# Two token tiles of batch 0 multiplied as a pair, by seven half-size products in place of two plain tiles

## The chip, the core and the metric

The kernel runs on one core of one Trainium2 chip. The metric is the device time of one execution in microseconds; the number given for a kernel is the median of several runs. Engines are called as the profile calls them: PE (TensorE, matrix products), PEld (its weight loads, which run beside it), DVE (VectorE), ACT (ScalarE), POOL (GpSimd) and SP (SyncE). POOL and SP also issue transfers (DMA). Each engine works through a queue of its own in order; where it needs something from another, it waits at that instruction, and all that is queued behind it waits too.

## The reference

There are four batches of 768 tokens. Each goes through a sparse attention of 8 heads of width 64, whose result is a row of 512 numbers for each of the 3072 tokens; then through a feed-forward part with 2048 inner numbers:

```python
# attention, per head (S=768, D=64): near keys within 16 tokens, and one summary key per block of 32
k_sum = k.reshape(B, H, nb, 32, D).max(axis=3)
v_sum = v.reshape(B, H, nb, 32, D).mean(axis=3)
scores_all = concat([where(|i-j| < 16, q @ k.T / sqrt(D), -1e9), q @ k_sum.T / sqrt(D) + log(32)])
a = softmax(scores_all)
attn = a @ concat([v, v_sum])
# feed-forward
x = attn as (3072, 512)
h = x @ w_in                                  # (3072, 2048)
g = h * (1 / (1 + exp(-1.702 * h)))
out = g @ w_out                               # (3072, 512)
```

## The kernel before, in words

The work goes in units. Batch 0 is two units of 384 tokens each (its two halves), batches 1 to 3 are one unit each. For a unit the kernel first forms the inner numbers: 16 ff tiles of 128 inner numbers each (`ff_in` for batch 0, lines 640 to 647), four matrix products of 128x128 by 384 tokens for each tile, then the gelu on ACT, which writes a row `nt` of `gT`. A batch has 6 token tiles of 128 tokens; the left half holds three, the right half the other three. Then it forms the output: for each token tile all 16 rows of `gT` times `w_out`.

Two ways of forming the output are in the kernel. `ff_out` (lines 848 to 859) is the plain one: 16 products of 512 columns into one PSUM bank `po`, in four parts of four products; ACT copies the bank to SBUF (`osb`) and SP stores it. `product` (lines 760 to 824) is used for batches 1 to 3: a pair of token tiles (one left, one right) is taken together, in seven steps of eight products of 256 columns each instead of the eight that four quarter blocks would need (Strassen's scheme in Winograd's form). It needs sums and differences of the two tiles' inner numbers, `gs` (four of them, made by `g_sums`, lines 668 to 675), and of the blocks of `w_out`, `ws` (`w_sum`, lines 679 to 686). The seven go to three banks `poA`, `poC` and `poB`. Between them intermediate values are copied out (`s1` after product 1, `s5` after 5, `s2` after 6), and later results are a bank plus such a copy, added on DVE into `osb` (after products 2, 7 and 3); the last quarter is a copy by ACT (after product 4). Product 6 goes on adding onto the bank that `s1` was copied from, 7 onto the one that `s2` was copied from, and 4 onto the one that the sum of 7 was read from, so each has to wait for that copy or sum.

The stage of interest is batch 0's right half (its second unit), lines 1079 to 1096. While its ff tiles are formed (line 1083 on), a table `todo` puts work for batch 1's attention in between: `tk` and `tq` transpose keys and queries on PE (the key copies go to ACT, the query copies to DVE; a key's maxima `ks` are reduced on DVE and spread by POOL in `rest_k`), `w_sum` forms parts of `ws` on DVE, and `value_rows(1)` at the end sums the value blocks on PE into two banks `ps_vs`, from which DVE makes `vs`. Then come 12 slots (line 1090): each is a part of `ff_out`, and then what `plan1` lists for that slot of batch 1's attention: `s` scores of one head pair and the exponential on ACT, `m` the mask on DVE, `v` values and their norms on DVE, `x` transposes of the result, `t` the query transposes t2 and t3, `g` a switch of ACT's table. Two digits name the half and the head pair or group. In slot 2 POOL is given batch 2's loads, after slots 9 and 11 SP is given transposing loads of keys (`xk`).

All instructions are kept in the order of the program on each engine (class `_Ordered`, lines 18 to 32), so no planner moves them; what the framework still chooses is which free bank a tile gets and which waits are set. PSUM has eight banks: the pool `pmm` has four, used by ff tiles, `po`, the `poA`-like banks, query transposes, `ps_vs` and batch 1's values (two for each group); the pool `psb` has two double ones, for scores, key transposes and the result's transposes.

The lines that the change touches are 668 to 675 (a neighbour is added), 760 to 824, the table `plan1` in lines 1010 to 1012 and lines 1083 to 1096. The order of ff tiles named in it, `order2`, is the one that the later batches use: 0, 8, 1, 9, and so on (line 649).

Of the kernel before, what the change touches and what calls it, by code (L numbers as in the profile page):

```python
# [13 lines left out]
ALU = mybir.AluOpType  # L14
# [21 lines left out]
def kernel(  # L36
# [15 lines left out]
    d_model, d_ff = moe_w_in.shape  # L52
# [6 lines left out]
    NT = d_ff // 128  # L59
    HALF = S // 2  # L60
    TH = NQ // 2
    JH = NJ // 2

    pe = _Ordered(tc, nc.tensor)
    dve = _Ordered(tc, nc.vector)
# [139 lines left out]
    gTb = keep.tile([128, NT, S], F16, name="gT")  # L205
# [48 lines left out]
    def copy(eng, out, in_):  # L254
        if eng is act:
            act.activation(out=out, in_=in_, func=ACT.Copy)
        elif eng == "dve_alone":

            dve.tensor_reduce(out=out, in_=in_.unsqueeze(len(in_.shape)), axis=AX.X, op=ALU.max)
        else:  # L260
            eng.tensor_copy(out=out, in_=in_)
# [278 lines left out]
    def tk(p, s, eng):  # L540
        ps = psb.tile([128, 2048], BF16, name="ps_t", tag="big")[:, 0:S]
        turn_tiles(ps, kb2[p // 2][:, p % 2], NJ)
        copy(eng, at(flat_kx(p, s), 0, [[256, NJ], [192, 2], [1, 64]]),
             ps.rearrange("p (j e c) -> p j e c", e=2, c=64))
        rest_k(p, s, pool)
# [82 lines left out]
    def gelu(half, nt, ph):  # L628
        act.activation(out=gT[half][:, nt, :], in_=ph, func=ACT.Gelu_apprx_sigmoid)
# [3 lines left out]
    def ff_step(ph, half, nt, steps=range(KO)):  # L633
        for n in steps:
            g, i = n // 2, n % 2
            ko = g + 2 * i if halves[0] else 2 * g + i
            pe.matmul(out=ph, lhsT=w_in_sb[:, ko, nt * 128:(nt + 1) * 128],
                      rhs=xTT[half][g][:, i], start=(n == 0), stop=(n == KO - 1))

    def ff_in(half, nts):  # L640

        phs = [pmm.tile([128, HALF], F32, name="ph", tag="mm") for nt in nts]
        for part in ((0, 1), (2, 3)):
            for nt, ph in zip(nts, phs):
                ff_step(ph, half, nt, part)
        for nt, ph in zip(nts, phs):
            gelu(half, nt, ph)

    order2 = [nt for j in range(NT // 2) for nt in (j, j + NT // 2)]
# [18 lines left out]
    def g_sums(j, eng=dve, which=(0, 1, 2, 3)):  # L668
# [3 lines left out]
        for w in which:  # L672
            a, b_, op = {0: (a1[:, r], a2[:, r], ALU.add), 1: (gs[:, 0, j], a1[:, l], ALU.subtract),
                         2: (a1[:, l], a1[:, r], ALU.subtract), 3: (a2[:, l], gs[:, 1, j], ALU.subtract)}[w]
            eng.tensor_tensor(out=gs[:, w, j], in0=a, in1=b_, op=op)

    N1 = d_model // 2

    def w_sum(what, part):

        n = NT // 2
        c = slice(part * n // 2, (part + 1) * n // 2)
        w1, w2 = w_out_sb[:, 0:n], w_out_sb[:, n:]
        b11, b12, b21, b22 = w1[:, c, 0:N1], w1[:, c, N1:], w2[:, c, 0:N1], w2[:, c, N1:]
        a, b = {0: (b12, b11), 1: (b22, ws[:, 0, c]), 2: (b22, b12), 3: (b21, ws[:, 1, c])}[what]
        dve.tensor_tensor(out=ws[:, what, c], in0=a, in1=b, op=ALU.subtract)
# [31 lines left out]
    def last_bank(tag, name):  # L718
        return plast[tag in "AB"].tile([128, 512], F32, name=name, tag="last" + tag,
                                       bufs={"A": 3, "E": 2, "B": 1, "C": 2}[tag])  # L720
# [36 lines left out]
        gelu("CBAE".index(bank) % 2, j + (NT // 2 if bank in "AE" else 0), ff_now[j, bank])  # L757


    def product(b, t, what):  # L760
        n = NT // 2
        l = slice(t * 128, t * 128 + 128)
        r = slice(HALF + t * 128, HALF + t * 128 + 128)
        lo, hi = slice(0, N1), slice(N1, d_model)
        raw_l, raw_r = gTb[:, :, l], gTb[:, :, r]
        w1, w2 = w_out_sb[:, 0:n], w_out_sb[:, n:]
        lhs, rhs, bank, opens = {
            1: (raw_l[:, 0:n], w1[:, :, lo], "A", True),
            2: (raw_l[:, n:], w2[:, :, lo], "C", True),
            6: (gs[:, 1, :, l], ws[:, 1], "A", False),  # L770
            5: (gs[:, 0, :, l], ws[:, 0], "B", True),
            7: (gs[:, 2, :, l], ws[:, 2], "A", False),
            3: (gs[:, 3, :, l], w2[:, :, hi], "B", False),
            4: (raw_r[:, n:], ws[:, 3], "A", False)}[what]
        if opens:
            now[t, bank] = (last_bank("B" if bank == "A" and t == 2 else {"A": "A", "B": "E", "C": "C"}[bank],
                                      "po" + bank) if b + 1 == B
                            else pmm.tile([128, 512], F32, name="po" + bank, tag="mm"))
        po = now[t, bank][:, 0:N1]
        for i in range(n):  # L780
            pe.matmul(out=po, lhsT=lhs[:, i], rhs=rhs[:, i], start=(opens and i == 0),
                      stop=(i == n - 1), skip_group_check=True)

        def keep_it(name):
            if b + 1 == B and name == "s1":
                t_ = now[t, name] = spare[:, 2 * HALF + t * N1:2 * HALF + (t + 1) * N1]
            else:
                t_ = now[t, name] = snap.tile([128, N1], F32, name=name, tag=name)
            copy(dve if t == 0 and b + 1 < B else act, t_, po)

        def give(o, cols, name):
            if (t, o) not in now:
                now[t, o] = outp.tile([128, d_model], F32, name="osb", tag="osb")
            if name:
                dve.tensor_tensor(out=now[t, o][:, cols], in0=po, in1=now[t, name], op=ALU.add)
            else:
                act.activation(out=now[t, o][:, cols], in_=po, func=ACT.Copy)

        def store(o, tok, cols=slice(0, d_model)):
            r0 = b * S + tok  # L800
            sp.dma_start(out=out[r0:r0 + 128, cols], in_=now[t, o][:, cols])
            if cols.start == 0:
                now.pop((t, o))

        last = b == B - 1 and t == JH - 1

        if what == 1:
            keep_it("s1")
        elif what == 2:
            give("o1", lo, "s1")  # L810
        elif what == 6:
            keep_it("s2")
        elif what == 5:
            keep_it("s5")
        elif what == 7:
            give("o2", hi, "s5")
            if last:
                store("o2", HALF + t * 128, hi)
        elif what == 3:
            give("o1", hi, "s2")  # L820
            store("o1", t * 128)
        else:
            give("o2", lo, None)
            store("o2", HALF + t * 128, lo if last else slice(0, d_model))

    seq = [(0, 1)]
    for t in range(JH):
# [20 lines left out]
    def ff_out(u, ms, part):  # L848
        if part == 0:
            po_now[ms] = pmm.tile([128, d_model], F32, name="po", tag="mm")  # L850
        po = po_now[ms]
        for nt in range(4 * part, 4 * part + 4):
            pe.matmul(out=po, lhsT=gT[u % 2][:, nt, ms * 128:(ms + 1) * 128],
                      rhs=w_out_sb[:, nt, :], start=(nt == 0), stop=(nt == NT - 1))
        if part == 3:
            osb = outp.tile([128, d_model], F32, name="osb", tag="osb")
            act.activation(out=osb, in_=po, func=ACT.Copy)
            r0 = u * HALF + ms * 128
            sp.dma_start(out=out[r0:r0 + 128, :], in_=osb)
# [10 lines left out]
    def exp_soon():  # L870
        act.activation(out=gate[:, 1:2], in_=gate[:, 0:1], func=ACT.Exp)
# [120 lines left out]
    for e in range(2):  # L992
        r = slice(64 * e, 64 * e + 64)
# [5 lines left out]
    for p in range(NP):  # L999
# [9 lines left out]

    plan1 = {-1: ["s00", "s01"], 1: ["t2", "m00", "m01"], 2: ["t3", "s02"], 3: ["s03", "m02"], 4: ["m03", "s10"],  # L1010
             5: ["s11", "m10"], 6: ["v00", "m11", "s12", "s13"], 7: ["v01", "g"], 8: ["m12", "m13"],
             9: ["x00", "x01", "v10"], 10: ["v11"], 11: ["x10"]}

    plan = {-1: ["s00", "s01"], 2: ["m00", "m01"], 3: ["s02", "s03"], 5: ["m02", "m03", "s10", "s11"],
            7: ["m10", "m11", "s12", "s13"], 9: ["m12", "m13"], 10: ["v00", "v01"], 11: ["d00"],
# [52 lines left out]
    gs = snap.tile([128, 4, NT // 2, HALF], F16, name="gs")  # L1068
    ws = keep.tile([128, 4, NT // 2, N1], F16, name="ws")
    exp_soon()  # L1070
    beside0(-1)
    for i, (ms, part) in enumerate((ms, part) for part in range(4) for ms in range(JH)):
        ff_out(0, ms, part)
        beside0(i)
        if i in (10, 11):
# [3 lines left out]
    todo = {3: [lambda: tk(0, 1, act)], 4: [lambda: w_sum(2, 0)], 5: [lambda: tk(1, 1, act)],  # L1079
            6: [lambda: w_sum(2, 1)], 7: [lambda: w_sum(3, 0)], 8: [lambda: tk(2, 1, act)],   # L1080
            10: [lambda: w_sum(3, 1)], 9: [lambda: tq(0, 1, dve)], 11: [lambda: tk(3, 1, act)], 12: [lambda: tq(1, 1, dve)],
            15: [lambda: value_rows(1)]}
    ff_in(1, range(3))
    for nt in range(3, NT):
        ff_in(1, (nt,))
        for f in todo.get(nt, ()):
            f()
    exp_soon()
    beside(1, -1)
    for i, (ms, part) in enumerate((ms, part) for ms in range(JH) for part in range(4)):  # L1090
        ff_out(1, ms, part)
        beside(1, i)
        if i == 2:
            load_batch(2)
        if i in (9, 11):
            xk(i // 2 - 4, 0)


# [1 line left out]
    for b in range(1, B - 1):  # L1100
# [32 lines left out]
        i = 0  # L1133
# [16 lines left out]
    b, n = B - 1, NT // 2  # L1150
# [25 lines left out]
    for slot in range(7 * (n - PLAIN)):  # L1176
# [3 lines left out]
        for j in range(PLAIN, n):  # L1180
            for what in steps.get(slot - 7 * (j - PLAIN), ()):
                ff_do(j, what)
    ff_do(n - 2, "A")
    product(b, 0, 1)
    ff_do(n - 1, 7)
    ff_do(n - 1, "c")
# [45 lines left out]
```

## Time and profile before

| | before |
|---|---|
| time, median of 3 runs | 208.15 us (207.64 to 208.67) |
| span of the profiled execution, first to last instruction | 205.6 us |
| granted TensorE clock in it | 1.000 |
| PE busy | 198.5 us, 97% |
| DVE busy | 139.9 us, 68% |
| ACT busy | 123.7 us, 60% |
| POOL busy | 93.5 us, 45% |

The profile gives no time of its own for the profiled execution beside the span; the median of the runs is 2.55 us above that span.

How to read it: the profile is of one execution. A line of the order of time gives start, duration from the first start to the last end of a merged group, engine, operation, what is written and from what, and the count. Starts are from the first instruction on. Successive matrix products overlap, so a group's pace is read from starts and not from the durations of single products. A value in square brackets is the time for which the engine stood idle before the group, and what released it. The chain that ended last gives 90% of its time to PE.

### The profile page before, as it was taken

Reading aid. Unit: us, or ns where it says so; the run is one execution under the profiler, and the core shown is the slowest. Engines: PE = TensorE matmul, PEld = TensorE weight load, DVE = VectorE, ACT = ScalarE, POOL = GpSimd, SP = SyncE. Lnnn points to the kernel's source line nnn. Section 1 sums busy time; section 2 is a strip of 40 time slices with the busy share of each in tenths; the row PEclk is TensorE's granted clock in tenths of the full one; section 3 lists DMA queues with packets and bytes.
Section 4 is the critical chain, followed back from the end, with each engine's and each line's share of the span. In section 5 each row is a group of like instructions: output and inputs, shape, how many; then the busy total and the mean of one; then the engine's idle time right before and its main releaser. Section 6 shows DMA issues by size and latency. Waiting matters only on the chain.

```text
span 205.6 us, 5854 instructions
## 1 busy us (share of the span) xinstructions
PE 198.5 (97%) x2364; PEld 138.1 (67%) x2364; DVE 139.9 (68%) x388; ACT 123.7 (60%) x237; POOL 93.5 (45%) x145
## 2 busy tenths in 40 slices
PE   7889999999999999999999999999999999999992
PEld 7658564556754566565888875566888865668882
DVE  4767795594856793898757789896769546758221
ACT  2374975728885716677772446778670577983220
POOL 7976289645899585000977036000000019990000
PEclk9999999999999999999999999999999999999999
DMA  5999999999999999999999989999023640000223
GB/s 59 153 158 198 207 212 207 204 156 233 124 145 153 177 170 135 163 145 141 139 180 158 164 162 136 130 248 154 0 105 86 149 126 3 0 0 3 102 102 105
DMA packets 97131, 27.74 MB, mean 135 GB/s; under 512 B 86720, under 2 KB 94160, under 8 KB 97104
## 3 DMA queue, kind: packets, MB, share of 16 engines
q0 software_dynamic: 71472, 13.64, 90.7%
q1 hardware_dynamic: 25632, 13.74, 32.3%
q8 instruction: 18, 0.29, 0.7%
q14 instruction: 9, 0.07, 0.1%
HBM read 27.26 MB, written 6.29 MB: 163 GB/s over the span
## 4 chain that ended last, share of the span: by engine, by line
PE 90%; DMA 4%; POOL 3%; issue 1%; DVE 1%; ACT 0%; POOLq 0%; DVEq 0%
PE ph L28 33%; PE poA L28 16%; PE po L28 11%; PE poB L28 8%; PE ps_av L28 4%; DMA v0n<-in_v_dram 4%; PE poC L28 4%; PE phA L28 4%; PE ps_s L28 3%; PE ps_t L28 1%; POOL kb L28 1%; PE ps_x L28 1%; PE phB L28 1%; PE phC L28 1%; PE phE L28 1%; PE ps_vs L28 1%
## 5 line engine op out<-in xcount | busy, mean ns | idle before, releaser
L28 PE MATMUL ph<-xT,w_in_sb 128*128 128x384 f16 x416 | 70.2, 326 | 0.1
L28 PEld LDWEIGHTS <-w_in_sb 128*128 128x128 f16 x452 | 43.7, 98 | 27.8 <-issue 0.2
L28 ACT ACTIVATE gT<-ph 128x384 f16<-128x384 f32 x104 | 49.8, 491 | 18.5 <-PE ph L28 18.2
L28 PEld LDWEIGHTS <-gT 128*128 128x128 f16 x312 | 28.8, 98 | 11.0
L28 ACT ACTIVATE a_sb<-ps_s 128x768 bf16<-128x768 f32 (+1 forms) x32 | 25.0, 826 | 12.7 <-PE ps_s L28 12.7
L28 PEld LDWEIGHTS <-gs 128*128 128x128 f16 x288 | 27.7, 98 | 3.4
L28 POOL DMA_DIRECT2D vw<-in_v_dram x36 | 24.5, 694 | 12.0 <-DMA kb<-in_k_dram 6.3
L28 POOL TENSOR_TENSOR gs<-gT 128x384 f16<-128x384 f16 x9 | 8.2, 909 | 42.4 <-ACT gT L28 42.4
L28 PE MATMUL po<-w_out_sb,gT 128*128 128x512 f16 x96 | 23.6, 380 | 0.0
L28 DVE TENSOR_TENSOR a_sb<-a_sb,mk 128x768 bf16<-128x768 bf16 x28 | 14.9, 555 | 6.5 <-ACT a_sb L28 5.9
L28 PE MATMUL poA<-ws,gs 128*128 128x256 f16 x144 | 18.7, 273 | 0.0
L28 DVE TENSOR_TENSOR x<-ps_av,rc 128x384 f16<-128x384 f32 x32 | 17.8, 558 | 1.1
L28 DVE TENSOR_TENSOR gs<-gT 128x384 f16<-128x384 f16 (+1 forms) x34 | 13.4, 393 | 7.2 <-ACT gT L28 6.9
L28 POOL DMA_DIRECT2D qb<-in_q_dram x18 | 16.6, 936 | 1.9 <-DMA w_in_sb<-in_moe_w_in_dram 1.2
L28 POOL DMA_DIRECT2D kb<-in_k_dram x16 | 15.3, 970 | 1.2 <-POOLq L1216 0.8
L28 PEld LDWEIGHTS <-kx 64*128 64x128 bf16 (+1 forms) x372 | 9.4, 95 | 6.8 <-issue 4.4
L28 DVE TENSOR_REDUCE ks<-kx 128x24 bf16<-128x768 bf16 x12 | 11.4, 948 | 3.4 <-ACT kx L28 3.2
L28 ACT ACT_TABLE_LOAD x10 | 12.8, 1283 | 1.0 <-PEq L1216 0.8
L28 ACT ACTIVATE osb<-poA 128x256 f32<-128x256 f32 x9 | 3.5, 384 | 15.8 <-PE poA L28 15.8
L28 ACT ACTIVATE s<-poA 128x256 f32<-128x256 f32 x11 | 4.2, 385 | 11.2 <-PE poA L28 11.2
L28 PEld LDWEIGHTS <-a_sb 128*64 128x64 bf16 (+2 forms) x400 | 7.8, 108 | 2.8 <-issue 1.3
L28 PE MATMUL poA<-w_out_sb,gT 128*128 128x256 f16 x72 | 9.4, 273 | 0.0
(113 smaller groups left out, 281.4 us busy)
## 6 DMA issues: line engine op xcount, KB each, us to landing
out_dram<-osb SPq DMA_DIRECT2D x23, 256.0 KB, 3.7
kb<-in_k_dram POOLq DMA_DIRECT2D x16, 192.0 KB, 6.9
qb<-in_q_dram POOLq DMA_DIRECT2D x14, 192.0 KB, 9.2
vw<-in_v_dram POOLq DMA_DIRECT2D x36, 64.0 KB, 5.7
w_out_sb<-in_moe_w_out_dram POOLq DMA_DIRECT2D x4, 512.0 KB, 13.0
w_in_sb<-in_moe_w_in_dram POOLq DMA_DIRECT2D x3, 512.0 KB, 12.7
vw<-vs SPq DMA_DIRECT2D x6, 198.0 KB, 7.1
v0n<-in_v_dram POOLq DMA_DIRECT2D x4, 192.0 KB, 7.9
```

Of the source, the lines that this page charges most:

```text
L28: r = f(*a, **kw)
```

## The change

Batch 0's right half has three token tiles. Before, each is formed by `ff_out`. After, the last two (the fifth and sixth of the batch) are formed as a pair by `product` in seven steps, in the order 1, 2, 5, 6, 7, 3, 4, and then the first of the three by `ff_out` in four parts; that makes 11 slots for 12. `product` is given the two tiles' numbers, and reads the sums from columns 0 to 127 of `gs`. The sums come from a new function, `g_sums_tiles`, which forms all four for two rows and their partners at once; it is called on DVE behind ff tiles 5, 9 and 13 of the order and behind the first product. So that partners are there early, the ff tiles of this half are formed in the order `order2`. The slot of `x10` moves from 11 to 10, and `xk` from after slots 9 and 11 to after slots 8 and 10.

```diff
+    def g_sums_tiles(j, L, R, eng):
+        js, js2 = slice(j, j + 2), slice(j + NT // 2, j + NT // 2 + 2)
+        l, r = slice(L * 128, L * 128 + 128), slice(R * 128, R * 128 + 128)
+        o = [gs[:, w, js, 0:128] for w in range(4)]
+        for w, (a, b_, op) in enumerate(((gTb[:, js, r], gTb[:, js2, r], ALU.add), (o[0], gTb[:, js, l], ALU.subtract),
+                                         (gTb[:, js, l], gTb[:, js, r], ALU.subtract),
+                                         (gTb[:, js2, l], o[1], ALU.subtract))):
+            eng.tensor_tensor(out=o[w], in0=a, in1=b_, op=op)
...
-    def product(b, t, what):
+    def product(b, t, what, tiles=None):
         n = NT // 2
-        l = slice(t * 128, t * 128 + 128)
-        r = slice(HALF + t * 128, HALF + t * 128 + 128)
+        L, R = tiles or (t, JH + t)
+        l = slice(0, 128) if tiles else slice(t * 128, t * 128 + 128)
+        ll, r = slice(L * 128, L * 128 + 128), slice(R * 128, R * 128 + 128)
         lo, hi = slice(0, N1), slice(N1, d_model)
-        raw_l, raw_r = gTb[:, :, l], gTb[:, :, r]
+        raw_l, raw_r = gTb[:, :, ll], gTb[:, :, r]
...
-             9: ["x00", "x01", "v10"], 10: ["v11"], 11: ["x10"]}
+             9: ["x00", "x01", "v10"], 10: ["v11", "x10"]}
...
-    ff_in(1, range(3))
-    for nt in range(3, NT):
-        ff_in(1, (nt,))
-        for f in todo.get(nt, ()):
+    ff_in(1, order2[0:3])
+    for i in range(3, NT):
+        ff_in(1, (order2[i],))
+        for f in todo.get(i, ()):
             f()
+        if i in (5, 9, 13):
+            g_sums_tiles((i - 5) // 2, JH + 1, JH + 2, dve)
     exp_soon()
     beside(1, -1)
-    for i, (ms, part) in enumerate((ms, part) for ms in range(JH) for part in range(4)):
-        ff_out(1, ms, part)
+    steps1 = [("seven", what) for what in (1, 2, 5, 6, 7, 3, 4)] + [("plain", part) for part in range(4)]
+    for i, (kind, what) in enumerate(steps1):
+        if kind == "plain":
+            ff_out(1, 0, what)
+        else:
+            product(0, 1, what, (JH + 1, JH + 2))
+        if i == 0:
+            g_sums_tiles(6, JH + 1, JH + 2, dve)
         beside(1, i)
         if i == 2:
             load_batch(2)
-        if i in (9, 11):
+        if i in (8, 10):
             xk(i // 2 - 4, 0)
```

The stores inside `product` use `L * 128` and `R * 128` in place of `t * 128` and `HALF + t * 128`.

More of the change, by code (lines that the diff above doesn't have):

```diff
@@ L817, in product @@
             if last:
-                store("o2", HALF + t * 128, hi)
+                store("o2", R * 128, hi)
         elif what == 3:
             give("o1", hi, "s2")
-            store("o1", t * 128)
+            store("o1", L * 128)
         else:
             give("o2", lo, None)
-            store("o2", HALF + t * 128, lo if last else slice(0, d_model))
+            store("o2", R * 128, lo if last else slice(0, d_model))
     seq = [(0, 1)]
```

## The prediction

> **What bounds the kernel now.** I read three views: first the page's busy times, then the table of windows over the stage that the change touches, then the order of time of each engine in it. The page's first part:
>
> ```profile
> PE 198.5 (97%) x2364; PEld 138.1 (67%) x2364; DVE 139.9 (68%) x388; ACT 123.7 (60%) x237; POOL 93.5 (45%) x145
> ```
>
> TensorE (PE) is busy for 97% of the span of 205.6 us, so a microsecond taken from it or added as a wait in front of it counts nearly in full. The windows of the stage (window, its length, then busy time of PE, PEld, DVE, ACT, POOL):
>
> ```profile
> 52.30:58.30 6.00, 6.00 (x54) 3.98 (x51) 4.75 (x8) 4.68 (x10) 5.26 (x13) 1.00 1.81 117
> 67.90:72.10 4.20, 4.20 (x86) 2.45 (x86) 3.63 (x10) 3.28 (x4) 1.77 (x3) 1.00 2.14 187
> ```
>
> PE has no gap worth naming, at a granted clock of 1.00. VectorE (DVE) is the next engine: 4.75 of 6.00 us in the ff stage ahead, 3.63 of 4.20 us later. That is where added work can turn into waits. The order of time on PE (start, duration of the merged group, operation, count):
>
> ```profile
> 58.30 0.60 PE L28 MATMUL ps_vs<-vw,E 64*32 64x128 bf16 x48
> 59.30 1.90 PE L28 MATMUL po<-w_out_sb,gT 128*128 128x512 f16 x8
> 61.29 0.49 PE L28 MATMUL ps_t<-wide,qb 128*128 128x128 bf16 x6
> 62.91 0.35 PE L28 MATMUL ps_s<-qT,kx 64*128 64x64 bf16 x12
> 63.20 1.04 PE L28 MATMUL po<-w_out_sb,gT 128*128 128x512 f16 x4
> ...
> 74.81 1.04 PE L28 MATMUL po<-w_out_sb,gT 128*128 128x512 f16 x4
> 75.69 0.50 PE L28 MATMUL ps_x<-ident,x 128*128 128x128 f16 x6
> 76.02 1.46 PE L28 MATMUL ph<-xT,w_in_sb 128*128 128x384 f16 x8
> 81.65 0.60 PE L28 MATMUL ps_vs<-vw,E 64*32 64x128 bf16 x48
> ```
>
> A slot of four 512-wide products lasts 0.87 us (four starts of 0.217, worked out below; 74.81 to 75.69 is 0.88); a slot's twelve score products take 0.29 (62.91 to 63.20).
>
> **The change part by part.**
>
> *The products.* Out: two tiles of 16 products, 32 x 0.217 = 6.94 us. In: seven groups of eight 256-wide ones. Their price stands in the chain of the later batches, which do the same, and that of a 512-wide one in its row of least, median and greatest duration:
>
> ```profile
> 98.41 0.98 PE poA L28 x8
> 99.39 0.87 PE poB L28 x8
> ```
>
> ```profile
> L28 PE MATMUL po<-w_out_sb,gT x96: 379/379/390, 31.1 to 75.5; 128*128 128x512 f16 x96
> ```
>
> 0.87 us is 0.109 each, 56 x 0.109 = 6.10 us; after attention work a group takes 0.10 more (0.98), as plain slots do. So one half-size product costs as much as one slot of four plain ones; there are 11 slots for 12, and the gain is one slot: -0.88 us. The row of 59.30 gives 0.217 for 512 columns as (1.90 - 0.379)/7, that is 2.0 times the 256-wide price. The Trainium skill ("TensorE: Matmul & The Clock Gate", Back-to-back issue gap) gives sustained 131 ns at 512 columns and 81 ns at 128, by which 32 plain ones would cost 4.2 us, the 56 some 5.5 us (an estimate between its two figures), and the change would lose 1.3 us on PE alone; this trace shows 217 ns and contradicts it.
>
> *The sums on DVE ahead of the stage.* Four groups of four 256-element sums come in, three of them into the ff stage. The nearest rows are the same sums over 384 elements, and a 1024-element one for the slope:
>
> ```profile
> 80.98 0.36 DVE L28 TENSOR_TENSOR gs<-gT 128x384 f16<-128x384 f16 x1 [2.56 <-ACT gT L28]
> 81.37 0.36 DVE L28 TENSOR_TENSOR gs<-gs,gT 128x384 f16<-128x384 f16 x1
> 81.65 0.35 DVE L28 TENSOR_TENSOR gs<-gT 128x384 f16<-128x384 f16 x1
> 81.92 0.35 DVE L28 TENSOR_TENSOR gs<-gT,gs 128x384 f16<-128x384 f16 x1
> ```
>
> The ff stage of DVE now, which they join:
>
> ```profile
> 52.33 0.68 DVE L28 TENSOR_TENSOR ws<-w_out_sb 128x1024 f16<-128x1024 f16 x1
> 52.93 0.68 DVE L28 TENSOR_TENSOR ws<-w_out_sb,ws 128x1024 f16<-128x1024 f16 x1
> 53.75 0.95 DVE L28 TENSOR_REDUCE ks<-kx 128x24 bf16<-128x768 bf16 x1
> 54.62 0.55 DVE L28 COPY qT<-ps_t 128x768 bf16<-128x768 bf16 x1
> 55.08 0.68 DVE L28 TENSOR_TENSOR ws<-w_out_sb,ws 128x1024 f16<-128x1024 f16 x1
> 56.37 0.95 DVE L28 TENSOR_REDUCE ks<-kx 128x24 bf16<-128x768 bf16 x1 [0.60 <-ACT kx L28]
> 57.24 0.55 DVE L28 COPY qT<-ps_t 128x768 bf16<-128x768 bf16 x1
> 59.09 0.29 DVE L28 COPY vpart<-ps_vs 128x128 f32<-128x128 f32 x1 [1.30 <-PE ps_vs L28]
> 59.41 1.18 DVE L28 TENSOR_TENSOR vs<-ps_vs,vpart 32x128 bf16<-32x128 f32 x4
> ```
>
> From start to start a group of 384 is 0.39 + 0.28 + 0.27 + 0.27 = 1.21 us. 1024 elements start 0.60 apart and 384 start 0.27 apart, 0.52 ns an element, so 128 fewer save 0.066 each: 0.95 us a group. The first group goes in at 52.33, ahead of that row. DVE's spare time is 0.22 us before 53.75 (52.93 + 0.60) and 0.69 before 56.37 (55.08 + 0.60), so two groups leave it 1.90 - 0.91 = 0.99 us late at 57.24: the copy of the second q transposes ends at 58.78 instead of 57.79. The second ps_vs bank is that copy's bank (the program's list of waits has it so), and ps_vs is due at 58.30: it slips by about 0.5.
>
> *POOL beside them.* From 56.47 on POOL copies keys, the first and last of its rows:
>
> ```profile
> 56.47 0.74 POOL L28 COPY kx<-kx 128x80 bf16<-128x80 bf16 x3
> 60.30 0.43 POOL L28 COPY kx<-ks 128x288 bf16<-128x288 bf16 x1
> ```
>
> Near the end of the run stand two rows that show what that can do:
>
> ```profile
> 184.64 0.91 POOL L28 TENSOR_TENSOR gs<-gs,gT 128x384 f16<-128x384 f16 x1
> 185.09 0.67 DVE L28 TENSOR_TENSOR gs<-gT 128x384 f16<-128x384 f16 x1 [0.66 <-ACT gT L28]
> ```
>
> The same DVE sum, 0.36 alone, took 0.67 when it began inside a POOL operation and ended 0.21 after it. The sixteen POOL copies fill 56.47 to 60.73, 0.27 each. Six DVE operations with two inputs from SBUF now fall among them: the last of the second group, the 1024-wide one moved there from 55.08, and the third group's four. Each waits between 0 and a whole copy; I take half, 0.13, as nothing in the trace orders the two queues. That makes the copy end at 59.04 and ps_vs start at 59.07, the third group run from 58.95 to 60.43, vpart start at 60.43 (for 59.09), and vs give DVE back at 61.85 (0.32 and four of some 0.28 behind it). The fourth group, 0.95, ends at 62.80. The Trainium skill ("SBUF — State Buffer", Who interferes with whom) says that a DVE instruction with two SBUF inputs and a GpSimd instruction that reads SBUF exclude each other for the whole instruction; by that, the two alternate and every wait is nearer a whole copy, which is the second rival. The 0.67 row agrees.
>
> *The first result add stands ahead of the q copy.* On DVE the sum osb<-poC is queued before the copy of t2, which scores s02 need. Its other input, s1, comes from ScalarE (ACT) behind the two exponentials:
>
> ```profile
> 60.32 1.49 ACT L28 ACTIVATE a_sb<-ps_s 128x768 bf16<-128x768 f32 x2
> ```
>
> One copy and one add take (least, median and greatest duration in ns):
>
> ```profile
> L28 ACT ACTIVATE s<-poA x11: 383/384/392, 106.0 to 198.5; 128x256 f32<-128x256 f32 x11
> L28 DVE TENSOR_TENSOR osb<-poC,s x6: 418/424/426, 102.5 to 162.0; 128x256 f32<-128x256 f32 x6
> ```
>
> s1 is ready at 61.81 + 0.38 = 62.19, so the add can go at 62.23 at the earliest; with DVE's lateness it goes at 62.80, the copy runs from 63.14 to 63.70, s02 starts at 63.73. Before it was 62.91: **+0.82 us**. PE's own work would have reached s02 at about 63.6, so the waits at ps_vs (0.77) and here are one delay and not two, and the 0.25 for which PE stood before 61.29 is used up by it.
>
> *s03 and the chain over one bank.* Two masks and the copy of t3 follow on DVE (starts 0.46, 0.47, 0.47 apart, as above between 54.62 and 55.08), which ends at 65.09; s03 starts at 65.12 instead of 64.99. Product 7 adds onto the bank that s2 is copied from, and only s03 lies between 6 and 7: product 6 ends at 64.89, the copy runs from 65.10 to 65.48, product 7 starts at 65.51 instead of 65.28. **+0.23 us** for both. The later batches have product 2 in that place. Products 3 and 4 wait for nothing: their copies and adds (0.38 and 0.42) lie 1.2 us ahead.
>
> *One slot fewer at the end.* **-0.88 us**. But x10 now follows v11 at once. It needs the norms of v10:
>
> ```profile
> 74.47 0.56 DVE L28 TENSOR_TENSOR x<-ps_av,rc 128x384 f16<-128x384 f32 x1
> 75.85 0.56 DVE L28 TENSOR_TENSOR x<-ps_av,rc 128x384 f16<-128x384 f32 x1
> ```
>
> They end 75.03; x10 began at 75.69, and without the slot would at 74.81: **+0.25 us** of wait. The fourth ff bank of the next batch is then wanted at 76.37 and free with the last norm at 76.41: **+0.05**.
>
> *At nothing.* The order of ff tiles: same products, same widths. ACT's three copies and one eviction of 0.38 for two evictions of 0.60: it is idle for more than a fifth of the windows above (4.68 of 6.00, 3.28 of 4.20 us busy). POOL's queue keeps its order, SP's its count of stores (three); the key transposes move one slot earlier behind them. If loads and stores collide otherwise than now, it shows at 81.65, where the last value loads land:
>
> ```profile
> L28 POOL DMA_DIRECT2D vw<-in_v_dram x2: 684/690/697, 74.5 to 75.2; - x2
> DMA to landing us min/median/max: 6.7/6.9/7.1
> ```
>
> 75.2 + 6.7 = 81.9, and ps_vs, begun at 81.65, uses that row in its last sixth, at 82.0. With PE half a microsecond later, and POOL's copies, hence these loads, late by as much, I take 0, with up to 0.5 either way.
>
> **The sum**: 0.82 + 0.23 - 0.88 + 0.25 + 0.05 = +0.47 us. The span becomes 206.1; the page gives no time of its own for that execution beyond the span, and the median of the runs, 208.15, lies 2.55 above it, so 208.15 + 0.47 = 208.6.
>
> **The rivals.**
>
> *The waits are covered* (208.1). No contention with POOL: ps_vs at 58.81, vpart 59.64, the add at 62.23 as ACT allows, s02 at 63.15, +0.24 in place of +0.82, a sum of -0.11. For it: the POOL copies are short. Against: the 0.67 row.
>
> *DVE and POOL alternate* (209.5; slower). Each of the six operations waits a whole copy, 0.27: vpart 61.23, the add 63.6, s02 64.52, +1.61, a sum of about +1.3. It decides, that is passes half a per cent, from a mean wait of 0.22. A group price of 1.21, as at 384 elements, does it too with half the waits. For it: the 0.67 row; against: POOL's operation there was 0.91 long.
>
> *The whole slot is gained* (207.3). It needs every wait gone, and besides the loads: a PE earlier by 0.88 stands before the row that lands at 81.9 and keeps about 0.1 only, so that even a perfect stage would end near 208.0. That is the change not doing what it says, by a transfer, and I count it with the covered case.
>
> **How the numbers follow.** The forecast (208.3 to 209.1) has 0.45; covered, or given back at the loads, 0.28; alternation 0.22; the whole slot 0.05. The prediction is the likeliest, 208.6. Range 207.8 to 209.7: from the covered case less 0.3 of the runs' own spread up to the alternation. Half a per cent is 1.04 us, about what a measurement can tell: above 209.19 lies most of alternation and the top of the forecast, 0.22; below 207.11 hardly anything, 0.03; 0.75 between.
>
> **What would show it.** Right: seven half-size products at 0.87, the first ps_vs start near 59.1, DVE's osb<-poC near 62.8 followed by the q copy, PE idle before s02, before product 7 and before x10, and the next batch's first ph near 76.5 (76.02 + 0.47). The sums among POOL's copies should show durations over 0.30. Wrong: no idle at s02 (then DVE was not late, and 208.1 is nearer), ps_vs past 59.3 or a first ph past 77 (alternation), or a gap at the next ps_vs that outweighs the stage.

## The result and the profile after

The changed kernel is slower: the ratio to the kernel before is 1.0085 (95% interval 1.0065 to 1.0106), which on 208.15 us is 209.9. Over twenty runs of each on the same chips the medians are 210.08 us (207.96 to 214.12) and 207.84 us (206.78 to 209.87); the ratio leaves out a few executions that ran at a disturbed pace and are in these medians. On 207.84 us the ratio gives 209.6. The profiled execution took 209.56 us with a span of 207.9 us (205.6 before). The forecast was 208.6, in a range of 207.8 to 209.7, with 0.75 on "within half a per cent" and 0.22 on "slower"; 0.85% is outside that half per cent.

The page's first part and its shares of the chain that ended last, for the changed kernel:

```profile
PE 198.6 (96%) x2388; PEld 140.9 (68%) x2388; DVE 144.6 (70%) x407; ACT 124.2 (60%) x239; POOL 93.8 (45%) x145
PE 57%; DMA 20%; POOL 17%; issue 4%; DVE 0%; ACT 0%; POOLq 0%; DVEq 0%
```

PE is busy for 198.6 us, as before (198.5), in a span that is 2.3 longer: the loss is not more work for PE but waiting. The chain is no longer PE's alone; 20% of it is now transfers and 17% POOL. The chain in order of time says which (start, length, what):

```profile
56.15 2.95 POOL kx L28 x9
...
73.11 2.68 POOL vw L28 x4
75.79 8.40 DMA vw<-in_v_dram
...
84.23 0.25 PE ps_vs L28 x7
```

It goes from POOL's key copies through its loads to the last value load of batch 2, which takes 8.40 us to land, and only then to PE. Now the order of time on PE; the stage begins 0.27 us earlier in this execution (58.03 for 58.30), so 0.27 has to be added to compare with before:

```profile
58.03 0.23 PE L28 MATMUL ps_vs<-vw,E 64*32 64x128 bf16 x1
58.62 0.59 PE L28 MATMUL ps_vs<-vw,E 64*32 64x128 bf16 x47 [0.36 <-DVE qT L28]
...
62.92 0.49 PE L28 MATMUL ps_t<-wide,qb 128*128 128x128 bf16 x6 [0.19 <-DVE osb L28]
63.48 0.35 PE L28 MATMUL ps_s<-qT,kx 64*128 64x64 bf16 x12
...
64.79 0.35 PE L28 MATMUL ps_s<-qT,kx 64*128 64x64 bf16 x12
65.28 1.03 PE L28 MATMUL poA<-ws,gs 128*128 128x256 f16 x8
...
75.94 0.51 PE L28 MATMUL ps_x<-ident,x 128*128 128x128 f16 x6 [0.20 <-DVE x L28]
76.28 1.54 PE L28 MATMUL ph<-xT,w_in_sb 128*128 128x384 f16 x8
...
81.99 0.85 PE L28 MATMUL ps_vs<-vw,E 64*32 64x128 bf16 x41
84.23 0.25 PE L28 MATMUL ps_vs<-vw,E 64*32 64x128 bf16 x7 [1.39 <-DMA vw<-in_v_dram]
84.41 1.80 PE L28 MATMUL ph<-xT,w_in_sb 128*128 128x384 f16 x10
```

In the kernel before, ph goes on behind the second ps_vs (which begins at 81.65) at once:

```profile
82.18 0.66 PE L28 MATMUL ph<-xT,w_in_sb 128*128 128x384 f16 x3
```

From the first ps_vs to the next batch's first ph it is 76.28 - 58.03 = 18.25 us, for 17.72 before (76.02 - 58.30): the stage lost 0.53. The second ps_vs is reached 23.96 after the first (23.35 before), 0.61 late. Then its last seven products wait 1.39 us for value loads, and ph goes on 2.42 after ps_vs began, for 0.53 before (82.18 - 81.65): 1.89 more in one place. Together that is 2.50, and it stays to the end: the span from the first ps_vs on is 149.9, for 147.3. Three quarters of the loss is not in the stage that the change touches but 6 us behind it. (The ratio alone is worth 1.8 us, 0.85% of 207.84: the parts read from these two profiled executions add up to more than what the runs differ by.)

Two engines show the way there, DVE and POOL:

```profile
56.25 0.34 DVE L28 TENSOR_TENSOR gs<-gT,gs 128x256 f16<-128x256 f16 x1
56.51 0.73 DVE L28 TENSOR_TENSOR ws<-w_out_sb,ws 128x1024 f16<-128x1024 f16 x1
...
58.02 0.54 DVE L28 COPY qT<-ps_t 128x768 bf16<-128x768 bf16 x1
58.49 0.53 DVE L28 TENSOR_TENSOR gs<-gT 128x256 f16<-128x256 f16 x1
59.05 0.29 DVE L28 TENSOR_TENSOR gs<-gs,gT 128x256 f16<-128x256 f16 x1
59.26 0.34 DVE L28 TENSOR_TENSOR gs<-gT 128x256 f16<-128x256 f16 x1
59.52 0.42 DVE L28 TENSOR_TENSOR gs<-gT,gs 128x256 f16<-128x256 f16 x1
59.87 0.28 DVE L28 COPY vpart<-ps_vs 128x128 f32<-128x128 f32 x1
...
62.44 0.42 DVE L28 TENSOR_TENSOR osb<-poC,s 128x256 f32<-128x256 f32 x1
62.78 0.55 DVE L28 COPY qT<-ps_t 128x768 bf16<-128x768 bf16 x1
```

POOL's first load of batch 2 in the kernel before, then POOL in the changed one:

```profile
60.67 4.03 POOL L28 DMA_DIRECT2D kb<-in_k_dram  x4
```

```profile
56.15 1.30 POOL L28 COPY kx<-kx 128x80 bf16<-128x80 bf16 x3
...
58.82 0.98 POOL L28 COPY kx<-kx 128x80 bf16<-128x80 bf16 x3
...
61.24 4.04 POOL L28 DMA_DIRECT2D kb<-in_k_dram  x4
...
73.11 3.40 POOL L28 DMA_DIRECT2D vw<-in_v_dram  x5 [1.79 <-DMA kb<-in_k_dram]
```

The sums beside POOL's copies take up to 0.53 where they take 0.28 alone, as forecast. What the forecast named but took at nothing is the other side: three POOL copies took 0.74 before and take 1.30 and 0.98 beside sums, so POOL gives out batch 2's first load 3.21 after the first ps_vs (61.24 - 58.03), for 2.37 before (60.67 - 58.30). The 1.30 stands beside one sum of the pair and the 1024-wide sum of `w_out` parts, which the pair's sums pushed back from 55.08 to 56.51. SP's queue changed as well; its rows, the kernel before first, then the changed one:

```profile
64.94 6.23 SPq L28 DMA_DIRECT2D out_dram<-osb  x2
71.34 3.22 SPq L28 DMA_TRANSPOSE kx<-kb  x2
```

```profile
68.06 1.60 SPq L28 DMA_DIRECT2D out_dram<-osb  x2
69.84 3.57 SPq L28 DMA_TRANSPOSE kx<-kb  x2
```

Before, the first two tiles were stored 5.9 us apart (64.94 and 70.83). A pair's two tiles are finished together, so both 256 KB stores are issued within 1.3 us, and the transposing loads of keys follow 1.2 us sooner, counted from the first ps_vs (69.84 - 58.03 = 11.81, for 71.34 - 58.30 = 13.04). POOL's value loads are in flight among them. The last one left POOL 17.76 us after the first ps_vs (16.92 before) and took 8.40 us to land (6.73 before): 0.84 and 1.67 late.

### The profile page after: what moved, and what is told of

The parts are those of the page before. It is cut to its first block, busy times and chain, and to the rows that moved or that the text cites. A ratio compares the mean times of both kernels' runs of the same rounds, so it can differ in the third digit from the quotient of the medians.

```text
span 207.9 us, 5932 instructions
## 1 busy us (share of the span) xinstructions
PE 198.6 (96%) x2388; PEld 140.9 (68%) x2388; DVE 144.6 (70%) x407; ACT 124.2 (60%) x239; POOL 93.8 (45%) x145
## 3 DMA queue, kind: packets, MB, share of 16 engines
q0 software_dynamic: 71472, 13.64, 84.3%
## 4 chain that ended last, share of the span: by engine, by line
PE 57%; DMA 20%; POOL 17%; issue 4%; DVE 0%; ACT 0%; POOLq 0%; DVEq 0%
PE ph L28 20%; PE poA L28 16%; DMA vw<-in_v_dram 9%; PE poB L28 8%; DMA w_in_sb<-in_moe_w_in_dram 6%; DMA kb<-in_k_dram 5%; POOL vw L28 4%; PE poC L28 4%; PE phA L28 4%; POOL kb L28 3%; POOL kx L28 2%; POOL mk L28 2%; POOL v0n L28 2%; PE ps_s L28 2%; PE ps_av L28 2%
## 5 line engine op out<-in xcount | busy, mean ns | idle before, releaser
L28 PEld LDWEIGHTS <-gs 128*128 128x128 f16 x320 | 30.6, 98 | 4.0
L28 DVE TENSOR_TENSOR gs<-gT 128x384 f16<-128x384 f16 (+2 forms) x42 | 16.0, 380 | 8.4 <-ACT gT L28 8.1
L28 PE MATMUL poA<-ws,gs 128*128 128x256 f16 x160 | 20.8, 273 | 0.1
L28 PE MATMUL po<-w_out_sb,gT 128*128 128x512 f16 x64 | 15.5, 380 | 0.0
L28 ACT ACTIVATE s<-poA 128x256 f32<-128x256 f32 x13 | 5.0, 385 | 11.4 <-PE poA L28 11.4
L28 PE MATMUL poA<-w_out_sb,gT 128*128 128x256 f16 x80 | 10.4, 273 | 0.0
L28 PE MATMUL poA<-ws,gT 128*128 128x256 f16 x80 | 10.4, 273 | 0.0
```

The lines of the kernel that those rows point to most:

```text
L28: r = f(*a, **kw)
```

## The experiments

Three things could have delayed the value loads: POOL being late, the two stores side by side, the earlier transposing loads. POOL's lateness was tried alone in the kernel before; the other two were taken away, one at a time, from the changed kernel.

**The sums alone.** The kernel before, with plain tiles, the order of ff tiles and the sums, whose values nothing reads:

```diff
+        if i in (5, 9, 13):
+            g_sums_tiles((i - 5) // 2, JH + 1, JH + 2, dve)
...
         ff_out(1, ms, part)
+        if i == 0:
+            g_sums_tiles(6, JH + 1, JH + 2, dve)
```

> The kernel before, with the change's order of ff tiles and its four groups of sums on DVE at the same places, but all three token tiles still formed plainly (the sums are read by nobody). Theory A, that the sums block POOL's key copies, so that batch 2's loads are issued some 0.8 us late and PE waits for the last value row at the second ps_vs: the last value load lands near 82.8 instead of 81.9, PE waits there 0.4 to 0.8 us, ps_vs and s02 of the stage are late by about 0.5 and 0.1, and the kernel is 0.8 to 1.2 us slower than before. Theory B, that the loads are late because the pair's two stores are issued together at 68 us: no wait at the second ps_vs, only the stage's own 0.1 to 0.5 us.

Measured: 208.64 us, ratio 1.0022 (0.9983 to 1.0061). The sums delay the stage by themselves (in the profiled execution PE waited 0.7 us at the first ps_vs for DVE's query copy and 0.4 at the values for the block sums, `vw<-vs`, which are sent behind `vs`; the stage lost 1.4, more than the 0.1 to 0.5 expected, in an execution 0.9 above the median), but the second ps_vs began with all its rows there. So they do not make the loss by themselves: 0.46 us on 208.15, for the 1.8 of the change.

**POOL late alone.** The kernel before, with some 0.9 us of idle POOL copies ahead of batch 2's loads:

```diff
         if i == 2:
+            for _ in range(3):
+                pool.tensor_copy(out=idle_to, in_=mk[:, 2:4])
+            pool.tensor_copy(out=idle_to[:, 0, 0:1], in_=mk[:, 2, 0:1])
             load_batch(2)
```

> The kernel before, with four idle copies on POOL (together about 0.9 us) just ahead of batch 2's loads, and nothing else. Theory A: the loads are issued 0.9 us later, the last value load lands 0.9 later, near 82.8, PE waits for it 0.7 to 0.9 us, and the kernel is slower by as much. Theory B: the loads' landing is set by what shares the transfer engines, and a later issue is caught up on the way: within 0.3 us of before.

Measured: 207.95 us, ratio 0.9996 (0.9955 to 1.0038): no loss is shown. Yet the profiled execution of it, the order of time on PE, shows the wait:

```profile
82.70 0.21 PE L28 MATMUL ps_vs<-vw,E 64*32 64x128 bf16 x1 [0.64 <-DMA vw<-in_v_dram]
83.58 0.25 PE L28 MATMUL ps_vs<-vw,E 64*32 64x128 bf16 x7 [0.67 <-DMA vw<-in_v_dram]
```

That execution took 208.78 us, 0.8 above the median of its kernel. Loads that leave 1.4 us late can be too late, but the times of the ten runs do not show that as a rule. One profile is one execution; by the runs, lateness of this size alone does not bring the loss of the change (1.0085 lies far above the interval), though a loss of up to 0.8 us is not excluded.

**The stores behind.** The changed kernel, with the pair's two stores issued behind all of the stage's transposing loads instead of ahead of them:

```diff
+            if tiles:
+                t_ = now.pop((t, o))
+                later.append(lambda: sp.dma_start(out=out[r0:r0 + 128, cols], in_=t_[:, cols]))
+                return
...
+    for f in later:
+        f()
```

> The changed kernel, with the pair's two stores queued on SP behind the second transposing load of keys instead of behind products 3 and 4. Theory B: the value loads land again as before the change, the last near 82.7 (late only by POOL's 0.8), PE's wait of 1.4 at the second ps_vs shrinks to 0 to 0.4, and the kernel is 0.3 to 0.8 us slower than before instead of 1.8. Theory A alone: the wait stays at 1 us or more and the kernel stays 1.5 to 1.8 us slower than before.

Measured: 208.53 us, ratio 1.0023 (0.9987 to 1.0060). PE passes the second ps_vs without a stop:

```profile
83.03 0.60 PE L28 MATMUL ps_vs<-vw,E 64*32 64x128 bf16 x48
```

The answer for the last three value loads:

```profile
L28 POOL DMA_DIRECT2D vw<-in_v_dram x3: 684/697/709, 75.0 to 76.3; - x3
DMA to landing us min/median/max: 5.3/5.5/6.0
```

**The transposing loads behind.** The changed kernel, with the two transposing loads of slot 8 moved behind the last slot, next to the other two:

```diff
-        if i in (8, 10):
-            xk(i // 2 - 4, 0)
+        if i == 10:
+            xk(0, 0)
+            xk(1, 0)
```

> The changed kernel, with the first transposing load of keys queued behind slot 10, next to the second, instead of behind slot 8. If these transposes are what the value loads collide with (theory C), the last value load lands near 82.7 and PE's wait shrinks to 0 to 0.4 us; the kernel is then 0.3 to 0.8 us slower than before. By theories A and B nothing changes but a few tenths: 1.4 to 1.8 us slower than before.

Measured: 208.16 us, ratio 1.0014 (0.9981 to 1.0046). The order of time on PE and the answer for the last three value loads:

```profile
82.09 0.60 PE L28 MATMUL ps_vs<-vw,E 64*32 64x128 bf16 x48
```

```profile
L28 POOL DMA_DIRECT2D vw<-in_v_dram x3: 684/697/709, 73.6 to 74.9; - x3
DMA to landing us min/median/max: 3.7/4.0/4.3
```

The same answer for the changed kernel:

```profile
L28 POOL DMA_DIRECT2D vw<-in_v_dram x3: 699/709/719, 74.4 to 75.8; - x3
DMA to landing us min/median/max: 7.5/7.9/8.4
```

The flight of the loads is halved by where SP issues two other transfers. POOL was as late here as in the changed kernel (61.60 - 58.18 = 3.42 after the first ps_vs), and it did no harm.

**The changed kernel once more**, beside the next two:

> The changed kernel once more, on the chip of the two runs beside it, to compare them with: 0.5 to 1.0% slower than before, with a wait of PE for the last value load at the second ps_vs of about 1 us or more in its profile. If the wait is a matter of how the transfers happen to fall in a run, the profile may show less of it.

Measured: 209.61 us, ratio 1.0085 (1.0052 to 1.0117), the same ratio as the first time. Its profiled execution has the same wait (0.90, last landing at 84.64, flight 9.04).

**The sums out of POOL's way.** The changed kernel; one group of sums stays in the ff stage, the other three are formed behind vs, as four sums of 768 elements (`g_sums_rows(w, 2, ...)` forms sum w of rows 2 to 7 and their partners in one instruction):

```diff
-        if i in (5, 9, 13):
+        if i == 5:
             g_sums_tiles((i - 5) // 2, JH + 1, JH + 2, dve)
...
         if i == 0:
-            g_sums_tiles(6, JH + 1, JH + 2, dve)
+            for w in range(4):
+                g_sums_rows(w, 2, JH + 1, JH + 2, dve)
```

> The changed kernel with the sums of rows 2 to 7 formed behind vs in four longer operations instead of among POOL's key copies; stores, transposes and products as in the changed kernel. Theory A, that POOL's lateness is a needed part of the late landing: POOL's first load is issued 0.8 us earlier against ps_vs, ps_vs no longer waits for the q copy, the last value load lands no later than PE needs it, and the kernel is 0.3 to 0.6 us slower than before (s02, s03, product 7 and x10 as in the changed kernel). Theory D, that stores and transposes falling together are enough: the load still lands 0.5 us or more after PE needs it, and the kernel stays 1.2 us or more slower than before.

Measured: 208.60 us, ratio 1.0033 (1.0003 to 1.0063). Neither ps_vs waits now, and POOL gives out its last value load 16.1 us after the first ps_vs. But a new wait stands in the stage, in the order of time on PE: the add of product 2 is behind the long sums on DVE, and PE waits for its bank.

```profile
58.88 0.60 PE L28 MATMUL ps_vs<-vw,E 64*32 64x128 bf16 x48
...
63.67 0.49 PE L28 MATMUL ps_t<-wide,qb 128*128 128x128 bf16 x6 [0.67 <-DVE osb L28]
...
82.73 0.60 PE L28 MATMUL ps_vs<-vw,E 64*32 64x128 bf16 x48
```

The flight of the value loads was as long as in the changed kernel (the last took 7.9 us): they came in time because they left earlier, with 0.2 us to spare (landed 82.89; the last seven products, which need them, start some 0.3 us after 82.73). The wait went, as the first theory of the expectation said. But these loads left earlier than even those of the kernel before (16.12 us after the first ps_vs, for 16.92), and in the second execution of the changed kernel they left as early as before (16.89) and PE still waited 0.90. So the wait does not need a late POOL; sums out of its way give the loads a head start that makes up for the longer flight.

**Everything put right.** The sums behind vs and spread over slots 0, 2 and 3, the add of product 2 behind the query copy, s10 and x00 a slot earlier, v10 ahead of x01, the transposing loads behind the last slot:

```diff
+    plan1 = {-1: ["s00", "s01"], 0: ["W0", "W1"], 1: ["t2", "H", "m00", "m01"], 2: ["t3", "s02", "W2"],
+             3: ["s03", "m02", "s10", "W3"], 4: ["m03"],
+             5: ["s11", "m10"], 6: ["v00", "m11", "s12", "s13"], 7: ["v01", "g"], 8: ["m12", "m13", "x00"],
+             9: ["v10", "x01"], 10: ["v11", "x10"]}
...
+            elif what[0] == "W":
+                g_sums_rows(i, 2, JH + 1, JH + 2, dve)
+            elif what[0] == "H":
+                held.pop()()
```

> The changed kernel with each wait that its profile showed taken away: the sums of rows 2 to 7 behind vs, two of the four operations put behind the copies that PE waits for; the add osb<-poC behind the copy of t2; scores s10 between products 6 and 7; x00 one slot earlier and v10 ahead of x01; the first transposing load of keys behind slot 10. If the stage's terms are right (+0.8 at s02, +0.2 at product 7, +0.25 at x10, -0.88 for the slot) and the second ps_vs waits for no load, the next batch's first ph comes 0.4 to 0.7 us earlier than in the kernel before, counted from the first ps_vs's due time, and the kernel is 0.2 to 0.6 us faster than before (ratio 0.997 to 0.999). If PE's gain is given back at the loads or later, it is at 1.000.

Measured: 207.59 us, ratio 0.9990 (0.9960 to 1.0021). It ran again beside the next one:

> The kernel with everything shifted once more, on the same chip as the one with the transposes put back: both theories expect 0.998 to 1.000 of before, first ph of the next batch 1.0 us earlier against the first ps_vs than before, and the wait at the scores of batch 2 again.

Measured: 207.42 us, ratio 0.9990 (0.9959 to 1.0022). The order of time on PE of this second one:

```profile
58.68 0.60 PE L28 MATMUL ps_vs<-vw,E 64*32 64x128 bf16 x48
...
75.24 1.79 PE L28 MATMUL ph<-xT,w_in_sb 128*128 128x384 f16 x8
...
81.19 0.60 PE L28 MATMUL ps_vs<-vw,E 64*32 64x128 bf16 x48
```

The stage is 16.56 us long (16.65 the first time), 1.1 less than before and more than the 0.4 to 0.7 expected. In both profiles 0.3 of it is lost at the fourth ff bank, so 0.84 is left at the second ps_vs, and 0.7 at the end of this span (205.3 - 58.68 = 146.6, for 147.3). In the first profile 0.4 more was lost at the scores of batch 2, whose transposed queries SP issued at 92.61 (88.01 before) behind four transposing loads of keys. That wait was absent from the second profile, against what was expected, so it isn't a fixed price. Both medians lie below that of before, and both intervals hold 1: a gain isn't shown.

**The transposing loads put back.** The kernel just told, with one thing undone:

```diff
-        if i == 10:
-            xk(0, 0)
-            xk(1, 0)
+        if i in (8, 10):
+            xk(i // 2 - 4, 0)
```

> Like the kernel with everything shifted (sums behind the q copies, held add, scores a slot earlier, late transposes), but with the transposing loads of keys back behind slots 8 and 10. That kernel gained 1.07 us in the stage and gave back 0.31 at the fourth ff bank and 0.4 at the scores of batch 2, whose transposed queries were issued by SP at 92.61 (before: 88.01) behind four transposes of keys. Theory (SP's queue took the gain): the transposed queries are issued near 88 to 90, that wait goes, and the time is 0.4 us below the other's, some 207.2 where before stands at 207.7. Rival (the value loads take it instead): with the transposes early, batch 2's last value loads land past 83.4 on the other's scale, PE waits at the second ps_vs, and the time is at or above the other's, 207.6 to 208.5.

Measured: 208.67 us, ratio 1.0042 (1.0015 to 1.0068). The rival was right: the wait at the second ps_vs is back, as the order of time on PE and the answer for the last three value loads show:

```profile
81.25 0.53 PE L28 MATMUL ps_vs<-vw,E 64*32 64x128 bf16 x40
82.46 0.21 PE L28 MATMUL ps_vs<-vw,E 64*32 64x128 bf16 x1 [0.67 <-DMA vw<-in_v_dram]
83.61 0.25 PE L28 MATMUL ps_vs<-vw,E 64*32 64x128 bf16 x7 [0.94 <-DMA vw<-in_v_dram]
```

```profile
L28 POOL DMA_DIRECT2D vw<-in_v_dram x3: 699/709/719, 74.0 to 75.3; - x3
DMA to landing us min/median/max: 7.1/7.8/8.3
```

POOL was not late here (first load 60.69 - 58.62 = 2.07 after the first ps_vs, sooner than before's 2.37), and none of the pair's sums stood among its copies (three of them still took 1.20 us beside the sum of `w_out` parts). PE reached the second ps_vs 0.72 us earlier than before (22.63 for 23.35), and the last value load landed 1.3 later (24.95 for 23.64). The place of the transposing loads alone cost this kernel about 1 us (1.0042 for 0.9990; the intervals overlap between 1.0015 and 1.0022).

All the profiled executions in one table. Times in the second to fourth column are counted from the moment at which the first ps_vs was due; the fourth is when the second ps_vs began; "flight" is the last value load's issue to landing:

| | first load leaves | last value load leaves / lands | second ps_vs | flight | PE's wait there | ratio |
|---|---|---|---|---|---|---|
| before | 2.37 | 16.92 / 23.64 | 23.35 | 6.7 | 0 | 1 |
| after | 3.21 | 17.76 / 26.16 | 23.96 | 8.4 | 1.39 | 1.0085 |
| after, again | 2.88 | 16.89 / 25.94 | 24.21 | 9.0 | 0.90 | 1.0085 |
| sums alone | 2.79 | 17.11 / 24.51 | 24.77 | 7.4 | 0 | 1.0022 |
| POOL late | 3.74 | 18.30 / 25.11 | 23.09 | 6.8 | 1.31 | 0.9996 |
| stores behind | 2.80 | 17.76 / 23.08 | 24.47 | 5.3 | 0 | 1.0023 |
| transposing loads behind | 3.42 | 16.75 / 20.48 | 23.91 | 3.7 | 0 | 1.0014 |
| sums behind | 2.22 | 16.12 / 24.01 | 23.85 | 7.9 | 0 | 1.0033 |
| everything, 1st and 2nd | 1.85, 2.25 | 16.38 / 20.69, 15.70 / 19.88 | 22.60, 22.51 | 4.3, 4.2 | 0 | 0.9990 |
| transposing loads put back | 2.07 | 16.68 / 24.95 | 22.63 | 8.3 | 1.61 | 1.0042 |

The order on SP's queue sorts the flight: two stores and two transposing loads in a row ahead of the last value loads give 7.9 to 9.0 us; the stores taken away 5.3; the transposing loads taken away 3.7 to 4.3; the order of before 6.7 to 7.4. When POOL starts its loads does not sort the flight, but it counts for the landing, which is leaving plus flight. With SP's order as in the changed kernel, the loads of the kernel with sums behind left 1.64 us earlier and landed 2.15 earlier, and PE did not wait. Stores taken away, transposing loads taken away, or the sums out of POOL's way: each removed the wait, while the sums alone and POOL late alone did not bring the loss. SP's order was enough without a late POOL in the last row, where PE came 0.72 earlier than before, and in the second execution of the changed kernel; in the first, POOL's lateness added 0.84. The kernel before was not tried with SP's order changed and nothing else.

## Where the prediction was right and where it failed

*The stage: right in the profiled execution, within a spread.* With 0.27 added to the times of after: s02 at 63.75 (forecast 63.73), product 7 at 65.55 (65.51), first ph at 76.55 (76.5), the wait before x10 0.20 (0.25), the fourth ff bank 0.08 (0.05). The sums cost 0.93 us a group undisturbed (0.95). PE's wait stood before the transposes of t3 and not before s02, because their bank is the one that osb<-poC frees; they come just before s02 in PE's queue, and the +0.82 came out as +0.84. The stage lost 0.53 to its end and 0.61 to the next ps_vs, for +0.47. The kernels without the wait at the loads bear the size out: the changed kernel with the stores or the transposing loads behind is at +0.5 and +0.3 us (1.0023 and 1.0014 of 208.15). In the other profiled executions with the pair and these sums the stage lost 0.49 (transposing loads behind), 0.78 (after, again) and 1.04 (stores behind), the last with 0.17 of waiting for the block sums `vw<-vs`, a transfer that the prediction did not name. So the +0.47 is the lower part of what one execution can lose there.

*DVE and POOL: half waits, not alternation.* Six sums waited up to 0.25 each. The third group of sums took 1.45 us from first start to last end (58.49 to 59.94; forecast 58.95 to 60.43, 1.48). In the five profiles with these sums PE's wait at the first ps_vs was between 0.25 and 0.77, so how the two queues fall together changes from one execution to the next. The rival that ended near the measured time, alternation (209.5), did so for another reason: the two engines did not alternate.

*The loads: the step that failed.* "I take 0, with up to 0.5 either way" stood for the collision of loads and stores at the next ps_vs. It measured 1.89 us. The mechanism was named and its place was right, and "a gap at the next ps_vs that outweighs the stage" was listed as what would make the prediction wrong; the size was taken from the flight of before, 6.7 us, as though it belonged to the load. The runs show that it goes with what SP has in flight at that time: 3.7 to 9.0 us. The change moved three of SP's transfers there: counted from the first ps_vs, the first store went from 6.64 to 10.03 us, and the second store and the transposing loads came some 1.2 earlier (12.53 to 11.30, 13.04 to 11.81). "SP's count of stores (three)" was kept, but a pair gives its two stores at once. The rows of before held 0.1 us of room at this place (landing 81.9, used at 82.0): lateness there is paid almost one for one, and POOL's loads were 0.84 late in leaving and 1.67 longer in flight.

*The chances.* That the loads could cost more than the stage was nowhere in the sum of chances; slower had its 0.22 from alternation and the top of the forecast. The time lies at the upper end of the range, 209.7: just inside with 209.6, just past it with 209.9. That it is so near is luck, since the range's end came from an alternation that did not happen. The rows of before could have given a wider bound: the twelve value loads of this batch took between 5.2 and 8.3 us there, so that a last load of 8.3 in place of 6.7 would have been 1.6 late.

What stays open: by which means stores and transposing loads lengthen the flight of value loads from another engine's queue (nothing here measures one of them by itself against a quiet machine), and why the kernel with POOL late waits in its profile while its times show no loss.

## What to carry to other kernels

A stage's own sum can be right and the time still go elsewhere: for every transfer that lands with less room than its flight can vary, look up which other transfers the change moves next to it, on every queue, and bound the flight by that and not by its present value. When results are finished in pairs their stores come in pairs too; move the transfers that nobody needs soon (here transposing loads) behind the ones that PE waits for. A slower neighbour is two-sided: work put on DVE beside POOL's copies delays what POOL issues afterwards.

## What the runs showed of the hardware

- The flight of a 64 KB value load from POOL's queue was between 3.7 and 9.0 us for the same load at the same place in the program, by what SP had issued around it: moving two transposing loads behind it took 8.4 to 3.7, moving two 256 KB stores behind took 8.4 to 5.3. Each is the flight in one profiled execution; two executions of the changed kernel gave 8.4 and 9.0.
- POOL stood still over its own transfers: before the last five value loads it waited 1.79 us until an earlier key load (kb) had landed. The waits of POOL's loads in this stage end 0.28 us after the landing of the load eight before: the fourth key load landed at 72.83 and the eighth value load left at 73.11 (before: 72.07 and 72.35). So lateness of one load is handed on to later ones. Whether the chip or the program's own waits ask for this, no run here shows.
- In one execution (transposing loads put back) the granted clock stood at 0.50 from 84.3 to 87.5 us, just behind PE's wait: 41 products of 384 columns began between 83.8 and 92 us, where the kernel with POOL late, after a wait of the same kind and at a clock of 1.00, began 51. The wait itself lies ahead of that stretch.
- DVE sums and POOL copies slow each other: 0.28 to 0.53 us for a 256-element sum, 0.74 to 1.30 for three POOL copies (0.98 beside sums of the pair alone, 1.20 beside the 1024-wide sum alone). The Trainium skill ("SBUF — State Buffer", Who interferes with whom) says that GpSimd's ports are DVE's second pair and that the lock on it is exclusive; both directions of these numbers agree, though the two did not alternate one for one.
